# Another order of products in an attention kernel's inner unit, with each key difference placed behind the reader of the one before

## The chip, the core and the metric

The kernel runs on one core of a Trainium2 chip. A core has TensorE (PE: matrix products into PSUM, with its weight loads shown apart as PEld), VectorE (DVE), ScalarE (ACT), GpSimd (POOL) and SyncE (SP, which here issues the DMAs). The engines run their own instruction queues in order and wait for each other at semaphores. The metric is the device time of one execution in microseconds (us), lower is better. A time before is the median of several executions; the profile comes from one more, of which the span from the first to the last instruction is shown.

## What is computed

Four attention layers follow each other on `x` of 2048 tokens by 576 channels, with a layer norm before each and the input added after each. Layers 0 and 2 (kind A) have 32 heads of width 18 with their own keys and values; layers 1 and 3 (kind B) have 32 query heads on one shared key and value.

```python
def _A_ref(x, wqkv, wo):
    qkv = (x @ wqkv).reshape(B, S, 3, H, Dh).transpose(2, 0, 3, 1, 4)
    q, k, v = qkv[0], qkv[1], qkv[2]
    scores = jnp.einsum("bhqd,bhkd->bhqk", q, k) * (Dh ** -0.5)
    p = _softmax(scores, axis=-1)
    o = jnp.einsum("bhqk,bhkd->bhqd", p, v)
    return o.transpose(0, 2, 1, 3).reshape(B, S, D) @ wo
# _B_ref: the same with k = x @ wk and v = x @ wv shared by all heads
x = A_x
x = x + _A_ref(_layernorm(x), A_wqkv, A_wo)
x = x + _B_ref(_layernorm(x), B_wq, B_wk, B_wv, B_wo)
x = x + _A_ref(_layernorm(x), A_wqkv, A_wo)
x = x + _B_ref(_layernorm(x), B_wq, B_wk, B_wv, B_wo)
```

## The kernel before

Each layer projects queries, keys and values, then runs a long attention loop, then the output projection. The attention is done for 16 pairs of heads `p` and 4 blocks `u` of 512 queries, so 64 parts (p, u) per layer and 256 in all. One part needs three kinds of work:

- **Maxima.** 32 products of 128 queries by 512 keys (two heads `a`, four query chunks `qc`, four key blocks `kb`), made by `max_mm` (PE L601). VectorE reads each from PSUM and takes the maximum over the keys (L606). The softmax needs the maximum of each query over all keys; `max_final` (L797) joins them, GpSimd splits the negative in two, and it goes by DMA into two extra rows of the queries.
- **Exponentials.** 32 products of 128 keys by 512 queries, made by `exp_mm` (PE L822), now with the maximum subtracted by the extra rows. ScalarE reads each from PSUM and writes the exponential to a tile `pt` (L826).
- **PV.** Four of these tiles at a time are multiplied with the values into the accumulator `oacc` (PE L864); when all 32 are in, ScalarE copies `oacc` to `oc` (L873).

A **key difference** shares a maximum between two key blocks. For key blocks 0 and 1, max(s0, s1) = s0 + max(s1 - s0, 0). So `max_mm` makes a product with the difference of the two blocks' keys (PE L590), ScalarE takes its relu (L599) and writes it to the one SBUF tile `relu`, and later the product of key block 0 is read by VectorE together with that tile (L604, followed by a short read of its accumulator): sum and maximum in one instruction. This instruction is the **reader** of the difference. It takes one pass off VectorE and gives one to ScalarE, three times per part. There is one `relu` tile, so the next relu may be written only when the reader of the last is done.

The heads of a pair lie in different halves of the array's rows: `q` and `k` are sliced from partition 64 a. Products of different heads that follow each other can run side by side.

**The order** is written out by hand in the table `UNIT`. One pass through its ten rows is a unit, with 32 exponentials and 32 maxima; it runs over and over, across the parts, since the maxima run `LEAD` = 14 steps of four ahead of the exponentials. An item is a letter, a head and a rank: `m` a plain maximum, `r` a key difference, `e` an exponential. The number after a row is how many columns of PV follow the row's products; 512 columns are one step. PV is 928 columns behind (`PV_LAG`).

```python
while m_done[0] < 4 * ns:
    rows, cols = UNIT[phase % len(UNIT)]
    run_todo(LEAD + sum(e_next) / 4)
    for kind, a, rank in rows:
        if kind == "e":
            exp_next(a, rank)
        elif m_done[0] < 4 * ns:
            max_mm(oldest(rank))
    ...
    pv_cols(cols - skip)
```

**Banks.** Beside `oacc` there are seven PSUM banks. `lru` holds them in the order of their last use, and `oldest(rank)` takes the one that was used longest ago (rank 0), or the next (1, 2). A product can start only when the last reader of its bank is done: ScalarE for `e` and `r`, VectorE for `m`. So each item's place and rank also say for which engine, and how far back, PE waits.

**Who reads which difference.** `m_order` fills the 16 maxima of a head in a part: the reader of a difference is the first plain maximum of the same head that stands more than three maxima behind it. Maxima are numbered 0 to 31 in a unit, differences included. Counted so, the table before has differences 13 (row 5, head 1), 18 (row 6, head 0) and 27 (row 9, head 1), with readers 17 (row 6), 22 (row 8) and 31 (row 10).

Other work is issued between the rows by `run_todo`, by how many exponentials have been issued: the transpose of the maxima (L806) and its DMAs, the sums and the division of the output on GpSimd, the loads of the next heads and of weights. `slot` picks a `pt` tile out of a ring of 14; `wrote` and `seen` are its account at build time of which ScalarE writes PE has already waited for, and steer that choice so that an exponential needs few waits.

Of the kernel before, what the change touches and what calls it, by code (L numbers as in the profile page):

```python
# [61 lines left out]

UNIT = [("m10 e00 e00 m10 m01 e10", 448),
# [9 lines left out]
UNIT = [([(o[0], int(o[1]), int(o[2])) for o in rows.split()], cols) for rows, cols in UNIT]  # L75
PV_LAG = 928
UNIT_M = [(kind, a) for rows, _ in UNIT for kind, a, _ in rows if kind != "e"]
assert len(UNIT_M) == 32 and sum(cols for _, cols in UNIT) == 4096


@with_exitstack
def tile_kernel(ctx: ExitStack, tc: tile.TileContext, A_x, A_wqkv, A_wo, B_x, B_wq, B_wk, B_wv, B_wo, out):
# [69 lines left out]
    def bank(i, name):  # L152
        lru.remove(i)
        lru.append(i)
        return psum.tile([P, 512], F32, tag=f"b{i}", bufs=1, name=name)
# [255 lines left out]
    for layer in range(4):  # L411
# [125 lines left out]
        def ops(p):  # L537
            return big[:, q_slot(p)], big[:, k_slot(p)]
# [11 lines left out]
        for a in range(2):  # L550
            n = -4 * LEAD % 32
# [10 lines left out]
        def max_place(a, i):  # L562

            p, u = divmod(i // 16, 4)
            if i < len(m_first):
                return (0, *m_first[i])
            n = i % 16
            return (p, u, *m_order[a][n]) if i >= 32 else (p, u, n // 2 % 4, n // 8 % 2 * 2 + n % 2)
# [5 lines left out]
        def max_mm(bank=mtile):  # L574

            i = m_done[0]
            a = m_heads[i]
            p, u, qc, kb = max_place(a, m_next[a])
            q, k = ops(p)
            if (p, u) not in mxs:  # L580
                mxs[p, u] = pool.tile([P, 32], F32, name="mx") if (p, u) < (0, 2) else mx2[u % 2]
            mx, ps = mxs[p, u], bank("psm")
            by_act = reader[lru[-1]]
            reader[lru[-1]] = False
            b, r = 64 * a, 16 * a + 4 * qc + kb
            c0 = u * 512 + qc * P
            if (p, u) >= (0, 2) and (a, qc, kb) in m_diff:
                assert kd_pair[p % 2 if is_a and p else 2] == (p if is_a else 0)
                k = kd(p)[b:b + 3 * DH]
                nc.tensor.matmul(ps.rearrange("p (h t) -> p h t", h=2) if p == 0 or not is_a else ps,  # L590
                                 q[b:b + 3 * DH, c0:c0 + P], k,
                                 start=True, stop=True)
                t = relus[p, u, a, qc] = relu[:, :512]
                reader[lru[-1]] = True
                if not by_act:
                    seen[0] = max(seen[0], wrote.get("relu", -1))
                wrote["relu"] = ticks[0]
                ticks[0] += 1
                nc.scalar.activation(t, ps, AF.Relu)  # L599
            else:  # L600
                nc.tensor.matmul(ps, q[b:b + KM, c0:c0 + P], k[b:b + KM, kb * 512:(kb + 1) * 512], start=True, stop=True)  # L601
                if kb == 0 and (p, u, a, qc) in relus:
                    t = relus.pop((p, u, a, qc))
                    nc.vector.tensor_tensor_reduce(t, ps, t, 1.0, LOWEST, OP.add, OP.max, mx[:, r:r + 1])  # L604
                else:
                    nc.vector.reduce_max(mx[:, r:r + 1], ps, axis=AX.X)  # L606
            m_next[a] += 1
            m_done[0] += 1
            while m_full and i >= m_full[0][1] + 2:
                max_final(*m_full.pop()[0])  # L610
            m_count[p, u] = m_count.get((p, u), 0) + 1
            if m_count[p, u] == 32:
                assert m_next[0] == m_next[1]
                m_full.append(((p, u), i))

        relus, diffs, kd_pair = {}, {}, {}
        ring, free, wrote, seen, ticks = [], [], {}, [-1], [0]

        def kd(p):
            if p == 0 or not is_a:  # L620
                return big[:, 1::4, 7 * 256:]
            i = p % 2
            return xx_flat[:, 512 * i:512 * i + 512]
# [43 lines left out]
        def max_pairs():  # L667

            if is_a:
                run_todo(m_done[0] // 4)  # L670
            elif m_done[0] == 44:
                max_store(0, 0)
            elif m_done[0] == 48:
                max_rows(0, 0)
            for i in range(4):
                max_mm(etile if i == 3 else mtile)
            while m_full:
                max_final(*m_full.pop()[0])
# [116 lines left out]
        def max_final(p, u):  # L795
            neg = pool.tile([P, 8], F32, name="neg")
            nc.vector.tensor_reduce(neg, mxs.pop((p, u)).rearrange("p (b k) -> p b k", k=4), axis=AX.X, op=OP.max,  # L797
                                    negate=True)
            hl = nms[p, u] = hls[(4 * p + u) % 2]
            copy(nc.gpsimd, hl[:, 0:8], neg)  # L800
            nc.gpsimd.tensor_tensor(hl[:, 8:16], neg, hl.bitcast(F32)[:, 0:8], op=OP.subtract)
# [109 lines left out]


        relu, raw = (pool.tile([P, 640], F32, tag="xh", bufs=2, name=n) for n in ("relu", "raw"))
        todo = {}

        def at(b, f, *args):
# [31 lines left out]
        def run_todo(st):  # L948
            for n in sorted(n for n in todo if n <= st):
                for f, args in todo.pop(n):  # L950
                    f(*args)
# [29 lines left out]
            skip = min(cols, PV_LAG - lagged)  # L981
            lagged += skip
            pv_cols(cols - skip)
            phase += 1
# [47 lines left out]
```

## Time and profile before

| | |
|---|---|
| median of 3 runs | 5727.78 us (5721.95 to 5728.45) |
| the profiled execution | 5725.34 us |
| its span | 5723.6 us |
| granted TensorE clock | 0.999 |
| busy share of the span | PE 98%, DVE 88%, ACT 84%, POOL 32% |
| one unit in layer 1 (2001.47 to 2020.59 us) | 19.12 us, PE 18.76, DVE 18.20, ACT 18.15 busy |

A row of the page's groups names the line, the engine and the operation, output and inputs by their names, the shapes and the count, then the busy time, the mean duration of one in ns, and the idle time before it with what ended it. Instructions of one kind overlap a little, so the busy time is less than count times mean. The view of waits says which engine waited at which line for whom: total, times, longest. The timeline has the start, the length, the engine and the line, with successive instructions of one group merged. A PE instruction's end is modelled.

### The profile page before, as it was taken

Reading aid. Unit: us, or ns where it says so; the run is one execution under the profiler, and the core shown is the slowest. Engines: PE = TensorE matmul, PEld = TensorE weight load, DVE = VectorE, ACT = ScalarE, POOL = GpSimd, SP = SyncE. Lnnn points to the kernel's source line nnn. Section 1 sums busy time; section 2 is a strip of 40 time slices with the busy share of each in tenths; the row PEclk is TensorE's granted clock in tenths of the full one; section 3 lists DMA queues with packets and bytes.
Section 4 is the critical chain, followed back from the end, with each engine's and each line's share of the span. In section 5 each row is a group of like instructions: output and inputs, shape, how many; then the busy total and the mean of one; then the engine's idle time right before and its main releaser. Section 6 shows DMA issues by size and latency. Waiting matters only on the chain.

```text
span 5723.6 us, 143368 instructions
## 1 busy us (share of the span) xinstructions
PE 5606.4 (98%) x55774; PEld 3067.1 (54%) x55774; DVE 5026.7 (88%) x9489; ACT 4831.2 (84%) x9624; POOL 1842.7 (32%) x2396
## 2 busy tenths in 40 slices
PE   9999999999999999999999999999999999999999
PEld 8644444444844444444686444444448444444446
DVE  4799999998699999999737999999977999999995
ACT  2599999999389999999626999999992999999996
POOL 3243333334233333323412433333342332323232
PEclk9999999999999999999999999999999999999999
DMA  6321111111421000000253211111114100000002
GB/s 204 120 59 41 42 46 44 43 44 27 130 62 26 23 24 20 21 23 24 60 172 102 55 46 41 44 44 46 38 38 132 51 24 23 24 24 20 23 15 79
DMA packets 276207, 303.69 MB, mean 53 GB/s; under 512 B 136270, under 2 KB 194214, under 8 KB 266238
## 3 DMA queue, kind: packets, MB, share of 16 engines
q1 hardware_dynamic: 275526, 294.53, 18.0%
q8 instruction: 438, 7.18, 0.5%
q14 instruction: 243, 1.99, 0.1%
HBM read 168.50 MB, written 121.95 MB: 51 GB/s over the span
## 4 chain that ended last, share of the span: by engine, by line
PE 85%; DVE 8%; ACT 3%; issue 2%; POOL 1%; DMA 0%; SPq 0%; ACTq 0%; POOLq 0%; DVEq 0%
PE oacc L864 33%; PE psm L601 21%; PE pse L822 19%; PE psn L259 6%; DVE mx L606 5%; PE psq L433 5%; ACT relu L599 3%; DVE relu L604 3%; PE psm L590 1%; ACT pt L826 0%; POOL ev L445 0%; PE ps L251 0%; DMA big<-qk_d 0%; POOL wsm L205 0%; PE oacc L252 0%
## 5 line engine op out<-in xcount | busy, mean ns | idle before, releaser
L826 ACT ACTIVATE pt<-pse 128x512 f32<-128x512 f32 x8192 | 4233.6, 620 | 104.8 <-PE pse L822 86.0
L606 DVE TENSOR_REDUCE mx<-psm 128x1 f32<-128x512 f32 x6704 | 4183.3, 684 | 81.6 <-PE pse L822 49.0
L601 PE MATMUL psm<-big 62*128 62x512 f32 x7448 | 2461.4, 430 | 91.5 <-ACT relu L599 88.8
L822 PE MATMUL pse<-big 64*128 64x512 f32 x8192 | 2537.5, 442 | 1.7 <-ACT evr L444 1.6
L864 PE MATMUL oacc<-pt,vbuf 128*19 128x416 f32 (+9 forms) x26544 | 1733.0, 368 | 4.6 <-DVE oc L176 4.0
L822 PEld LDWEIGHTS pse<-big 64*128 64x128 f32 x8192 | 1214.0, 184 | 796.8 <-DVE mx L606 370.6
L601 PEld LDWEIGHTS psm<-big 62*128 62x128 f32 x7448 | 1178.7, 185 | 687.2 <-ACT pt L826 251.9
L864 PEld LDWEIGHTS oacc<-pt,vbuf 128*19 128x19 f32 x26544 | 546.4, 97 | 792.4 <-issue 551.9
L176 POOL TENSOR_SCALAR hl<-neg 128x8 fp32r<-128x8 f32 x256 | 50.6, 197 | 2693.1 <-DVE neg L797 2693.1
L604 DVE CUSTOM_DVE_ANT_0 relu<-psm,relu 128x512 f32<-128x512 f32 x744 | 509.4, 685 | 175.7 <-ACT pt L826 173.6
L599 ACT ACTIVATE relu<-psm 128x512 f32<-128x512 f32 x744 | 452.1, 608 | 140.8 <-DVE mx L604 135.2
L864 PE MATMUL oacc<-pt,vy 128*19 128x384 f32 (+3 forms) x8176 | 570.1, 383 | 0.0
L892 POOL TENSOR_TENSOR rl<-lt,mone 128x8 f32<-128x8 f32 x256 | 422.3, 1650 | 297.6 <-DMA lt<-os 291.6
L176 POOL TENSOR_SCALAR os<-oc 32x512 f32<-32x512 f32 x512 | 313.2, 612 | 114.2 <-DVE oc L176 63.6
L441 ACT ACTIVATE ev<-psq 128x512 fp32r<-128x512 f32 (+1 forms) x112 | 66.9, 598 | 326.9 <-PE psq L433 222.8
L883 POOL TENSOR_TENSOR os<-os,oc 96x512 f32<-96x512 f32 x256 | 328.0, 1281 | 21.4
L905 POOL TENSOR_TENSOR os<-os,rb 96x512 f32<-96x512 f32 x256 | 328.7, 1284 | 18.9 <-DMA rb<-r_d 18.9
L259 PE MATMUL psn<-wsm,xx 128*128 128x288 f32 x2240 | 307.9, 296 | 1.3 <-issue 1.3
L259 PEld LDWEIGHTS psn<-wsm,xx 128*128 128x128 f32 x2240 | 298.7, 188 | 14.3 <-issue 12.3
L864 PEld LDWEIGHTS oacc<-pt,vy 128*19 128x19 f32 x8176 | 177.9, 98 | 229.4 <-issue 196.6
L447 DVE TENSOR_TENSOR ev<-psq,ev 128x512 fp32r<-128x512 f32 (+1 forms) x84 | 58.0, 691 | 213.9 <-ACT ev L441 202.6
L433 PE MATMUL psq<-yx,big 128*128 128x512 f32 (+2 forms) x826 | 197.1, 391 | 4.2 <-ACT yx L243 2.2
(93 smaller groups left out, 2391.5 us busy)
## 6 DMA issues: line engine op xcount, KB each, us to landing
big<-qk_d SPq DMA_DIRECT2D x172, 432.0 KB
qk_d<-ev SPq DMA_DIRECT2D x96, 512.0 KB
qk_d<-ev SPq DMA_DIRECT2D x120, 256.0 KB
rb<-r_d SPq DMA_DIRECT2D x512, 36.0 KB
o_d<-os SPq DMA_DIRECT2D x512, 36.0 KB
o<-o_d SPq DMA_DIRECT2D x64, 256.0 KB
xx<-qk_d SPq DMA_DIRECT2D x120, 72.0 KB
big<-m_d SPq DMA_DIRECT2D x512, 4.0 KB
```

The lines of the kernel that those rows point to most:

```text
L176: eng.tensor_scalar(dst, src, 1.0, 0.0, op0=OP.mult, op1=OP.add)
L259: nc.tensor.matmul(ps, lhs[:, xc, :], wsm[:, wc, h * 288:(h + 1) * 288], start=i == 0, stop=i == len(TERMS) - 1)
L433: nc.tensor.matmul(ps[:n].rearrange("p (u t) -> p u t", u=2)[:, us], w[:, wc, :n], xts[T][:, us, xc, :], start=(xc, wc) == TERMS[0], stop= ...
L599: nc.scalar.activation(t, ps, AF.Relu)
L601: nc.tensor.matmul(ps, q[b:b + KM, c0:c0 + P], k[b:b + KM, kb * 512:(kb + 1) * 512], start=True, stop=True)
L604: nc.vector.tensor_tensor_reduce(t, ps, t, 1.0, LOWEST, OP.add, OP.max, mx[:, r:r + 1])
L606: nc.vector.reduce_max(mx[:, r:r + 1], ps, axis=AX.X)
L822: nc.tensor.matmul(e, k[r:r + KE, kc * P:(kc + 1) * P], q[r:r + KE, u * 512:(u + 1) * 512], start=True, stop=True)
L826: nc.scalar.activation(pt, e, AF.Exp, scale=SCALE)
L864: nc.tensor.matmul(oacc[j:j + DH + 1, cs], v_of(kc)[:, 2 * p + a if is_a else 0, :], pts[p, u, i][:, cs], start=kc < 2 and c0 == 0, stop=k ...
L892: nc.gpsimd.tensor_tensor(rl, lts.pop((p, u)), mone, op=OP.pow)
L905: nc.gpsimd.tensor_tensor(t[:96], t[:96], rb[:96], op=OP.mult)
```

## The change

The table `UNIT` is replaced by another of ten rows. Items, ranks and PV columns stand differently; the differences are now 13 (row 5), 20 (row 7) and 28 (row 9), all of head 1. Around it, the one `relu` tile becomes a list of tiles that is taken in turn, with its account kept per tile; the list has one entry. An assertion at build time holds that a tile is not taken again before its reader has been issued.

```diff
@@ -62,16 +62,16 @@
 
 
 
-UNIT = [("m10 e00 e00 m10 m01 e10", 448),
-        ("m00 e11 e00 m10 e10 m01", 480),
-        ("e10 m01 e00 m10 m00 e10", 416),
-        ("e00 m11 m00 m10 e10 e01", 352),
-        ("e00 e10 m00 r12 m10 e01", 384),
-        ("m00 e10 e01 m10 m11 r00", 448),
-        ("e00 m10 e00 m01 e10 m01 e10", 416),
-        ("e10 m00 m10 m10 e00 e10 e00", 416),
-        ("m00 e10 e02 e10 m01 r10 m00", 352),
-        ("m11 e00 e10 m01 m10 e11 e00", 384)]
+UNIT = [("e00 m11 e10 e00 m00 m10", 416),
+        ("e00 e10 m00 m10 m01 e10", 512),
+        ("m10 e00 m01 e10 e10 m01", 384),
+        ("e10 m01 e10 e01 m10 e00", 320),
+        ("m00 e10 m00 r10 m00 e10", 448),
+        ("e00 m10 e00 m00 e10 m01 e10", 416),
+        ("e00 m10 e00 m10 r10 m00 e10", 416),
+        ("e00 m10 e00 m10 m10 e10 e00", 384),
+        ("e10 m00 m00 e00 m11 e00 r10", 416),
+        ("m10 e00 e11 m00 e11 m00", 384)]
 UNIT = [([(o[0], int(o[1]), int(o[2])) for o in rows.split()], cols) for rows, cols in UNIT]
 PV_LAG = 928
 UNIT_M = [(kind, a) for rows, _ in UNIT for kind, a, _ in rows if kind != "e"]
@@ -590,17 +590,20 @@
                 nc.tensor.matmul(ps.rearrange("p (h t) -> p h t", h=2) if p == 0 or not is_a else ps,
                                  q[b:b + 3 * DH, c0:c0 + P], k,
                                  start=True, stop=True)
-                t = relus[p, u, a, qc] = relu[:, :512]
+                j = turn_r[0] = (turn_r[0] + 1) % len(relu)
+                assert all(n != j for n, _ in relus.values())
+                t = relu[j][:, :512]
+                relus[p, u, a, qc] = j, t
                 reader[lru[-1]] = True
                 if not by_act:
-                    seen[0] = max(seen[0], wrote.get("relu", -1))
-                wrote["relu"] = ticks[0]
+                    seen[0] = max(seen[0], wrote.get(-1 - j, -1))
+                wrote[-1 - j] = ticks[0]
                 ticks[0] += 1
                 nc.scalar.activation(t, ps, AF.Relu)
             else:
                 nc.tensor.matmul(ps, q[b:b + KM, c0:c0 + P], k[b:b + KM, kb * 512:(kb + 1) * 512], start=True, stop=True)
                 if kb == 0 and (p, u, a, qc) in relus:
-                    t = relus.pop((p, u, a, qc))
+                    _, t = relus.pop((p, u, a, qc))
                     nc.vector.tensor_tensor_reduce(t, ps, t, 1.0, LOWEST, OP.add, OP.max, mx[:, r:r + 1])
                 else:
                     nc.vector.reduce_max(mx[:, r:r + 1], ps, axis=AX.X)
@@ -613,7 +616,7 @@
                 assert m_next[0] == m_next[1]
                 m_full.append(((p, u), i))
 
-        relus, diffs, kd_pair = {}, {}, {}
+        relus, diffs, kd_pair, turn_r = {}, {}, {}, [0]
         ring, free, wrote, seen, ticks = [], [], {}, [-1], [0]
 
         def kd(p):
@@ -911,6 +914,7 @@
 
 
         relu, raw = (pool.tile([P, 640], F32, tag="xh", bufs=2, name=n) for n in ("relu", "raw"))
+        relu = [relu]
         todo = {}
 
         def at(b, f, *args):
```

## Prediction

> **What bounds it.** The page comes first. No engine is free, and the chain that ended last runs through TensorE with a share on the other two.
>
> ```profile
> span 5723.6 us, 143368 instructions
> PE 5606.4 (98%) x55774; PEld 3067.1 (54%) x55774; DVE 5026.7 (88%) x9489; ACT 4831.2 (84%) x9624; POOL 1842.7 (32%) x2396
> PE oacc L864 33%; PE psm L601 21%; PE pse L822 19%; PE psn L259 6%; DVE mx L606 5%; PE psq L433 5%; ACT relu L599 3%; DVE relu L604 3%; PE psm L590 1%; ACT pt L826 0%; POOL ev L445 0%; PE ps L251 0%; DMA big<-qk_d 0%; POOL wsm L205 0%; PE oacc L252 0%
> L873 ACT ACTIVATE oc<-oacc 128x512 f32<-128x512 f32 x248 | 149.9, 605 | 0.7 <-issue 0.7
> ```
>
> ScalarE's copy `oc` comes once a unit: 248 units. The table by stretches, cut at five periods of the timeline, gives one: 19.12 us, of which PE 18.76, DVE 18.19 and ACT 18.16 are busy. That is 248 x 19.12 = 4742 us, four fifths of the span; only it changes.
>
> ```profile
> 2001.47:2020.59 19.12, 18.76 (x204) 9.24 (x201) 18.20 (x35) 18.15 (x38) 5.79 (x7) 1.00 0.05 11
> sum 95.60, PE 93.82 PEld 46.53 DVE 90.93 ACT 90.80 POOL 28.95; mean PE 18.76 PEld 9.31 DVE 18.19 ACT 18.16 POOL 5.79
> ```
>
> The view of waits says what the period contains beside work (us in total, times, longest):
>
> ```profile
> ACT relu L599 <- DVE mx L604: 135.2, 241, 0.6
> PE psm L601 <- ACT relu L599: 88.8, 244, 0.7
> DVE relu L604 <- ACT pt L826: 173.6, 246, 0.7
> ```
>
> All three fall about once a unit, so they are one event: ScalarE's relu waits 0.56 us for a VectorE reader, PE 0.36 us for that relu's bank, and VectorE then 0.71 us for PE. The timeline of one unit shows it:
>
> ```profile
> 2001.47 0.50 PE L601 MATMUL psm<-big 62*128 62x512 f32 x1
> 2002.01 1.29 DVE L606 TENSOR_REDUCE mx<-psm 128x1 f32<-128x512 f32 x2
> 2002.05 0.46 PE L590 MATMUL psm<-big 54*128 54x512 f32 x1
> 2003.22 0.68 DVE L604 CUSTOM_DVE_ANT_0 relu<-psm,relu 128x512 f32<-128x512 f32 x1
> 2003.33 0.50 PE L822 MATMUL pse<-big 64*128 64x512 f32 x1
> 2004.00 0.60 ACT L599 ACTIVATE relu<-psm 128x512 f32<-128x512 f32 x1 [0.56 <-DVE mx L604]
> 2004.65 0.50 PE L601 MATMUL psm<-big 62*128 62x512 f32 x1 [0.36 <-ACT relu L599]
> 2005.91 0.18 PEld L822 LDWEIGHTS pse<-big 64*128 64x128 f32 x1 [0.69 <-ACT pt L826]
> 2007.87 0.50 PE L601 MATMUL psm<-big 62*128 62x512 f32 x1
> 2009.73 0.50 PE L601 MATMUL psm<-big 62*128 62x512 f32 x1
> 2011.82 0.50 PE L601 MATMUL psm<-big 62*128 62x512 f32 x1
> 2011.82 0.50 PE L822 MATMUL pse<-big 64*128 64x512 f32 x1
> 2013.60 0.50 PE L601 MATMUL psm<-big 62*128 62x512 f32 x1
> 2015.44 0.49 PE L822 MATMUL pse<-big 64*128 64x512 f32 x1
> 2017.16 0.50 PE L822 MATMUL pse<-big 64*128 64x512 f32 x1
> 2018.91 0.50 PE L822 MATMUL pse<-big 64*128 64x512 f32 x2
> 2020.59 0.50 PE L601 MATMUL psm<-big 62*128 62x512 f32 x1
> ```
>
> The PE lines at 2001.47, 2003.33, 2005.91, 2007.87 and so on are the first products of the table's rows 6, 7, 8, 9, 10, 1, 2, 3, 4, 5 and again 6. Row 5's key difference (index 13) is read by index 17, the last maximum before row 6's key difference (18, at 2002.05). With one relu buffer, relu 18 must wait for reader 17, which has two maxima ahead of it on VectorE; row 7's index 21 (2004.65) takes relu 18's bank.
>
> **What a row costs PE without waits.** The two lines at 2011.82 show two products of different heads side by side; I count such a pair as one slot. Rows of 3 slots last 1.78 (row 1, 448 columns), 1.84 (row 2, 480) and 1.72 (row 3, 416); rows of 4 last 1.96 (row 8, 416) and 1.86 (row 9, 352). So 64 columns cost 0.10 to 0.12, a slot about 0.23. Rows 4 and 10 by the same steps are 1.61 and 1.91, row 5 is 1.68 as measured, row 6 equals row 1, row 7 equals row 8: together 18.10. The period's other 1.02 is waiting: row 7 lasts 2.58 (0.62 over), row 10 2.09 (0.18), row 4 1.75 (0.14), row 6 1.86 (0.08). Row 10's is the relu again, as ScalarE runs without a pause from 2004.00 until then. PE's idle 0.36 is therefore a poor measure of the loss; the rows give 0.62 to 0.80.
>
> **The change, part by part.** The Python edits around `relu` give a list of length one: same buffer, no new instruction, 0. The new table has the same ten rows, 32 exponentials, 26 plain maxima, 3 relus, 3 readers and 4096 columns, and counted by heads again 34 slots (six rows of 3, four of 4). So PE's floor stays 18.10, and so do the loads of DVE and ACT. All that changes is who waits for whom.
>
> Removed: the close reader. New key differences are 13, 20 and 28, all of head 1; by the order rule their readers are 18, 24 and, in the next unit, 0. The reader stands two products ahead of the next difference (18 before 20), then four (24 before 28), then thirteen; before it was one. Between row 6's start and relu 20, ScalarE has six exponentials; reader 18 has a transpose and three maxima ahead of it.
>
> Added: other bank waits. Four kinds of step decide them:
>
> ```profile
> 2004.49 5.58 ACT L826 ACTIVATE pt<-pse 128x512 f32<-128x512 f32 x11
> 2012.36 6.13 DVE L606 TENSOR_REDUCE mx<-psm 128x1 f32<-128x512 f32 x10 [0.19 <-PE pse L822]
> 2019.51 1.08 ACT L826 ACTIVATE pt<-pse 128x512 f32<-128x512 f32 x2 [0.24 <-PE pse L822]
> 2001.79 0.20 DVE L806 STREAM_TRANSPOSE tr<-hl 128x32 f32<-128x32 f32 x1
> 2018.40 0.17 DVE L797 TENSOR_REDUCE neg<-mx 128x8 f32<-128x32 f32 x1
> 2018.50 2.48 DVE L606 TENSOR_REDUCE mx<-psm 128x1 f32<-128x512 f32 x4
> ```
>
> ScalarE starts one item each (5.58 - 0.61)/10 = 0.497, call it 0.495 with relus; VectorE one maximum each (6.13 - 0.68)/9 = 0.606, a reader takes 0.68, the transpose 0.22 (2001.79 to 2002.01), `neg` 0.10 (2018.40 to 2018.50). A first product reaches ScalarE 0.59 after the row's start (2018.91 to 2019.51) and VectorE 0.54 after (2011.82 to 2012.36), later slots 0.23 each. A bank is free 0.05 after its reader ends (2004.60 to 2004.65). After a held last product the next row starts 1.26 later with 416 columns (2004.65 to 2005.91), so 0.57 plus the columns' 0.69.
>
> **The loop that is late next.** Set 0 where row 1's last product `m10` starts. Row 2 starts at 1.26, its first maximum at 1.26 + 0.54 + 0.23 = 2.03. From there VectorE has seven maxima and `neg` before row 4's `m10`, which starts at 2.03 + 7 x 0.606 + 0.10 = 6.37 and frees its bank at 7.10. Row 5's last product `e10` takes that bank. Row 4's last, `e00`, waits for row 3's last exponential too, behind the `oc` copy, so PE comes to row 5 at about 6.6 and would start `e10` at about 7.05. Row 6 starts at 7.10 + 0.57 + 0.75 (448 columns) = 8.42, and its first exponential at 9.01. Rows 6 to 10 give ScalarE 4, 4, 4, 4 and 3 items; the last starts at 9.01 + 18 x 0.495 = 17.92, ends 0.61 later, and its bank is free at 18.58. Row 1's `m10` takes it. So the unit can't be shorter than 18.58. Inside this loop row 9's `r10` waits for row 8's last exponential: by the same steps it holds PE by up to 0.13, and ScalarE's row 10 begins 0.04 to 0.10 later. I take **18.65**.
>
> The walk puts relu 20 at 11.93 + 0.05 and its reader's release at 11.77 + 0.05: a margin of 0.15, no wait. Relus 28 and 13 have over 1 us. PV of row 6 needs row 6's second exponential in its last 32 columns: 0.2 of margin. Table-driven DMA starts move by one row at most, and `neg` and the transpose stay in their rows; POOL, busy 5.79 of 19.12, covers this. If that cover went, one row's delay of an issue still lies under the 14 steps of lead. Waits that need a second semaphore cost an instruction on their own; their number in the new order is not known:
>
> ```profile
> L599 ACTq EVENT_SEMAPHORE  x492: 17/17/17, 228.4 to 5618.7; - x164
> L822 PEldq EVENT_SEMAPHORE  x506: 51/51/573, 214.3 to 5640.5; - x169
> ```
>
> One PE one more or less per unit is 0.05, both ends +-13 us; I take 0, and the range holds it.
>
> **Sum.** 19.12 - 18.65 = 0.47 per unit, times 248 = 117 us. The profiled execution took 5725.3 us (span 5723.6), between the runs of 5721.95 and 5728.45, 2.4 under the median. 5725.3 - 117 = 5609. A tenth of a us per unit is 25 us.
>
> **Rivals.**
> *Larger holds.* The same seven banks serve a tighter schedule, and 0.55 of holds may be 0.8 to 0.95 when several in a unit add (rows 4, 5, 7, 9 and 1 each show up to 0.2 in the walk). Period 18.9 to 19.05: 5671 to 5708. For it: the old table lost 0.22 in rows 4 and 6, away from the relu. Against: those holds lie on one loop and don't all add.
> *Nothing gained.* The wait is only handed to another reader of the same banks: 19.12, 5725. The Trainium skill, in "Perfetto Trace Analysis", section "Optimization Strategy", says that a gap which repeats on the engine that should be saturated can mean too few buffers. By that rule a new order with the same buffers would leave the 0.36. Against it stands the row at 2004.00, where a reader's place in the queue ends the wait, not a missing bank.
> *More.* All holds vanish and the busiest engine's 18.19 (DVE) to 18.4 decides: 19.12 - 18.3 = 0.82, 5522, or 5495 to 5547. Against: the 18.58 loop.
> *Slower.* Reader 18 comes late on VectorE. The margin is 0.15; ScalarE's next items feed row 8's last slot and row 9 without slack, so beyond the margin the period grows one for one, and passes 19.12 when the reader is 0.15 + 0.47 = 0.62 late, which is one maximum (0.606) more ahead of it. With relu 20 waiting the old 0.56 the unit takes 19.21: 5748. For it: VectorE is the fullest beside PE. Against: the order counted in the code.
>
> **Chances.** Forecast (18.45 to 18.85) 0.66; larger holds 0.12; nothing gained 0.06; more 0.08; slower 0.08. That is faster 0.86, same 0.06, slower 0.08, where 0.2% (11 us) is about what a measurement of this kernel tells from no change. The range, 5560 to 5685, runs from a period of 18.45 to 18.96: it takes in the semaphore instructions and half of the larger holds.
>
> **What would show it.** Right: relu's wait for DVE under 30 us in total (135.2 before), PE's for relu gone, a period near 18.65 in the table by stretches, DVE and ACT busy still 18.2, and PE or ACT waits left at rows 1, 4, 5 and 9. Wrong: a relu wait of about 0.5 per unit at row 7, or busy sums per unit that changed.

## The result, and the profile after

The changed kernel takes 5563.37 us (median of 4 runs, 5561.36 to 5564.3) against 5725.64 for the kernel before, measured with it: a ratio of 0.9716, 95% interval 0.97 to 0.9733. It is 162 us faster. The forecast was 5609, a gain of 117, with a range from 5560 to 5685.

From the page of the kernel before: the chain that ended last by engine, and the groups of the readers and of the relus.

```profile
PE 85%; DVE 8%; ACT 3%; issue 2%; POOL 1%; DMA 0%; SPq 0%; ACTq 0%; POOLq 0%; DVEq 0%
L604 DVE CUSTOM_DVE_ANT_0 relu<-psm,relu 128x512 f32<-128x512 f32 x744 | 509.4, 685 | 175.7 <-ACT pt L826 173.6
L599 ACT ACTIVATE relu<-psm 128x512 f32<-128x512 f32 x744 | 452.1, 608 | 140.8 <-DVE mx L604 135.2
```

From the page of the changed kernel: the span, the busy times, the same chain, and the same two groups (now L607 and L602).

```profile
span 5561.7 us, 139390 instructions
PE 5531.2 (99%) x53790; PEld 3103.8 (56%) x53790; DVE 5008.5 (90%) x9489; ACT 4808.8 (86%) x9624; POOL 1843.3 (33%) x2396
PE 95%; issue 1%; POOL 1%; DMA 1%; DVE 1%; SPq 0%; ACT 0%; POOLq 0%; ACTq 0%; DVEq 0%
L607 DVE CUSTOM_DVE_ANT_0 relu<-psm,relu 128x512 f32<-128x512 f32 x744 | 509.5, 685 | 38.0 <-PE psm L604 6.9
L602 ACT ACTIVATE relu<-psm 128x512 f32<-128x512 f32 x744 | 480.1, 645 | 1.4 <-DVE mx L607 0.7
```

The work of DVE and ACT is what it was (same counts, busy within 0.5%). Their shares of the chain fall from 8% and 3% to 1% and 0%; PE has 95% instead of 85%. The relus' idle time before them fell from 140.8 us to 1.4, the readers' from 175.7 to 38.0.

One thing did change in the work, which the prediction had put at nothing: PE runs 53790 matmuls instead of 55774, eight fewer a unit, since by the new columns fewer row ends cut a step of PV in two (16 pieces a unit instead of 17). A run below that has the old table's 55774 (two relu tiles) is as fast, so the gain doesn't come from that.

In the view of waits (total, times, longest) one relu waits for a reader instead of 241, and PE's wait for a relu is no longer there:

```profile
ACT relu L602 <- DVE mx L607: 0.7, 1, 0.7
```

The table by stretches gives two units of the changed kernel. One takes 18.45 us instead of 19.12, with DVE and ACT busy for 18.09 and 18.06:

```profile
2111.30:2129.75 18.45, 18.45 (x196) 9.43 (x192) 18.09 (x35) 18.06 (x37) 5.79 (x8) 1.00 0.05 11
2129.75:2148.20 18.45, 18.45 (x196) 9.42 (x192) 18.09 (x35) 18.06 (x37) 5.79 (x8) 1.00 0.15 36
```

19.12 - 18.45 is 0.67, and 248 units of it are 166 us; the profiled executions differ by 5725.34 - 5563.46 = 162. The missing 4 us were not followed up.

The timeline of the first of the two (start, length, engine and line) has the rows' first products and the few instructions that the text comes back to: reader 18 and relu 20 in row 7, the last exponentials of rows 10 and 3, row 1's `m10`, row 4's last exponential product, VectorE's first maximum of row 2 and its `m10` of row 4, and row 5's `e10` at 2130.33:

```profile
2111.30 0.50 PE L604 MATMUL psm<-big 62*128 62x512 f32 x1
2113.10 0.50 PE L825 MATMUL pse<-big 64*128 64x512 f32 x1
2115.07 0.50 PE L825 MATMUL pse<-big 64*128 64x512 f32 x1
2115.74 0.69 DVE L607 CUSTOM_DVE_ANT_0 relu<-psm,relu 128x512 f32<-128x512 f32 x1
2116.63 0.60 ACT L602 ACTIVATE relu<-psm 128x512 f32<-128x512 f32 x1
2117.06 0.49 PE L825 MATMUL pse<-big 64*128 64x512 f32 x1
2118.98 0.49 PE L825 MATMUL pse<-big 64*128 64x512 f32 x1
2121.00 0.50 PE L604 MATMUL psm<-big 62*128 62x512 f32 x1
2122.53 0.61 ACT L829 ACTIVATE pt<-pse 128x512 f32<-128x512 f32 x1
2122.69 0.49 PE L825 MATMUL pse<-big 64*128 64x512 f32 x1
2123.26 0.43 PE L604 MATMUL psm<-big 62*128 62x512 f32 x2
2124.45 0.50 PE L825 MATMUL pse<-big 64*128 64x512 f32 x2
2125.22 0.69 DVE L609 TENSOR_REDUCE mx<-psm 128x1 f32<-128x512 f32 x1
2126.34 0.50 PE L604 MATMUL psm<-big 62*128 62x512 f32 x1
2127.98 0.62 ACT L829 ACTIVATE pt<-pse 128x512 f32<-128x512 f32 x1
2128.01 0.50 PE L825 MATMUL pse<-big 64*128 64x512 f32 x1
2128.65 0.50 PE L825 MATMUL pse<-big 64*128 64x512 f32 x1
2129.51 0.68 DVE L609 TENSOR_REDUCE mx<-psm 128x1 f32<-128x512 f32 x1
2129.75 0.50 PE L604 MATMUL psm<-big 62*128 62x512 f32 x1
2130.33 0.41 PE L825 MATMUL pse<-big 64*128 64x512 f32 x1
```

The row starts at 2111.30, 2113.10, 2115.07, 2117.06, 2118.98, 2121.00, 2122.69, 2124.45, 2126.34, 2128.01 and 2129.75 are rows 5 to 10, 1 to 4 and again 5. They last 1.80, 1.97, 1.99, 1.92, 2.02, 1.69, 1.76, 1.89, 1.67 and 1.74. By the steps of the prediction these rows without waits would last 1.78, 1.96, 1.96, 1.91, 1.96, 1.67, 1.72, 1.89, 1.67 and 1.56, together 18.08. So 0.18 of hold is left in row 4, 0.06 in row 9 and no more than 0.04 elsewhere. Relu 20 starts 0.20 after its reader is done (2115.74 + 0.69 = 2116.43).

### The profile page after: what moved, and what is told of

It is laid out like the page before. It is cut to its first block, busy times and chain, and to the rows that moved or that the text cites. A ratio compares the mean times of both kernels' runs of the same rounds, so it can differ in the third digit from the quotient of the medians.

```text
span 5561.7 us, 139390 instructions
## 1 busy us (share of the span) xinstructions
PE 5531.2 (99%) x53790; PEld 3103.8 (56%) x53790; DVE 5008.5 (90%) x9489; ACT 4808.8 (86%) x9624; POOL 1843.3 (33%) x2396
## 3 DMA queue, kind: packets, MB, share of 16 engines
q14 instruction: 243, 1.99, 0.1%
## 4 chain that ended last, share of the span: by engine, by line
PE 95%; issue 1%; POOL 1%; DMA 1%; DVE 1%; SPq 0%; ACT 0%; POOLq 0%; ACTq 0%; DVEq 0%
PE oacc L867 37%; PE pse L825 28%; PE psm L604 16%; PE psn L259 6%; PE psq L433 5%; PE psm L590 2%; DVE mx L609 0%; POOL ev L445 0%; PE ps L251 0%; POOL wsm L205 0%; DMA raw<-in_A_wo_dram 0%; ACT pt L829 0%; DMA qk_d<-ev 0%; POOL big L205 0%; DMA big<-m_d 0%
## 5 line engine op out<-in xcount | busy, mean ns | idle before, releaser
L825 PE MATMUL pse<-big 64*128 64x512 f32 x8192 | 2605.8, 441 | 4.2 <-DMA big<-m_d 3.4
L604 PE MATMUL psm<-big 62*128 62x512 f32 x7448 | 2366.7, 432 | 4.1 <-ACT evr L444 1.6
L867 PE MATMUL oacc<-pt,vbuf 128*19 128x384 f32 (+10 forms) x25552 | 1733.9, 376 | 3.7 <-DVE oc L176 3.7
L825 PEld LDWEIGHTS pse<-big 64*128 64x128 f32 x8192 | 1162.0, 184 | 872.9 <-ACT pt L829 345.4
L867 PE MATMUL oacc<-pt,vy 128*19 128x288 f32 (+8 forms) x7184 | 569.0, 413 | 0.0
L607 DVE CUSTOM_DVE_ANT_0 relu<-psm,relu 128x512 f32<-128x512 f32 x744 | 509.5, 685 | 38.0 <-PE psm L604 6.9
L602 ACT ACTIVATE relu<-psm 128x512 f32<-128x512 f32 x744 | 480.1, 645 | 1.4 <-DVE mx L607 0.7
L867 PEld LDWEIGHTS oacc<-pt,vy 128*19 128x19 f32 x7184 | 154.5, 98 | 176.5 <-issue 132.8
```

Of the source, the lines that this page charges most:

```text
L825: nc.tensor.matmul(e, k[r:r + KE, kc * P:(kc + 1) * P], q[r:r + KE, u * 512:(u + 1) * 512], start=True, stop=True)
L867: nc.tensor.matmul(oacc[j:j + DH + 1, cs], v_of(kc)[:, 2 * p + a if is_a else 0, :], pts[p, u, i][:, cs], start=kc < 2 and c0 == 0, stop=k ...
```

## The experiments

The theory: the old table lost its time because one relu waited for the reader of the last, by the time at which VectorE's queue reached it. The rivals: the gain comes from the new order of banks, heads and columns; or what counts is how many products lie between reader and difference. Each ratio is to the kernel before, measured beside the run; its medians there lie between 5723.00 and 5727.19 us, so times of different runs compare to about 4 us.

**The old table, reader one maximum earlier.** Only the rule that picks readers is changed, in the kernel before.

```diff
-                order[min(j for j, (at_, x) in enumerate(own) if at_ > own[i][0] + 3 and not x and not order[j])] = qc, 0
+                order[min(j for j, (at_, x) in enumerate(own) if at_ > own[i][0] + 2 and not x and not order[j])] = qc, 0
```

> The kernel before with its old table; only the rule that picks readers is changed from more than three maxima behind to more than two. Reader 17 of difference 13 becomes 16, one maximum (0.61 us) earlier on VectorE; readers 21 and 31 as good as before. Table, banks, heads and PV columns are the old ones. Theory (the gain comes from the relu's wait for its reader): the wait of 0.56 per unit goes, with row 7's 0.62 and most of row 10's 0.18; unit 18.3 to 18.5 us, time 5530 to 5580, relu's wait for VectorE under 10 us. Rival (the gain comes from the new order of banks and heads, the wait is only handed on): unit above 18.9, time 5670 to 5725.

Measured: 5589.26 us (5587.66 to 5590.08), ratio 0.9761 (0.9746 to 0.9775). That is 135 of the 162 us, without the new table. It is 9 us above the expected range. In its timeline, the first line is the reader, the second ScalarE's item before the relu, the third the relu that had waited:

```profile
2125.32 0.68 DVE L604 CUSTOM_DVE_ANT_0 relu<-psm,relu 128x512 f32<-128x512 f32 x1
2125.51 0.64 ACT L826 ACTIVATE pt<-pse 128x512 f32<-128x512 f32 x1
2126.11 0.60 ACT L599 ACTIVATE relu<-psm 128x512 f32<-128x512 f32 x1
```

The relu starts 0.11 after its reader's end (2126.00), about the 0.10 of the old wait (2003.90 to 2004.00): it still starts as soon as its reader lets it. No idle time is listed, since it starts before the item ahead of it ends (2126.15). But it starts 0.60 after that item's start, where relu 20 of the changed kernel does so 0.48 after (2116.15 to 2116.63). That is some 0.12 lost in each unit, by estimate 30 us if all of it shows (248 x 0.12); the next run, without this wait, is 30.5 us faster.

**The old table with two relu tiles.** The code of the changed kernel, the old table, and a second tile.

```diff
-        relu = [relu]
+        relu = [relu, xx_flat[:, 4096:4608]]
```

> The old table with the old readers, and a second relu tile taken in turn (512 columns of a buffer that is idle in the attention loop; relus written there are rounded to its type, which changes the maximum that is subtracted in its last bits). Reader 17 stays directly ahead of difference 18, but relu 18 goes to the other tile. Theory (the wait is for the one tile's reader): the wait goes, unit 18.50 to 18.56 as with the reader one maximum earlier, time 5580 to 5600. Rival (the reader matters in another way than by the tile, for instance by the banks it holds): unit above 18.9, time over 5670.

Measured: 5558.74 us (5556.43 to 5562.13), ratio 0.9708 (0.9691 to 0.9724): as fast as the changed kernel, and 21 us under the lower expected end. The view of ScalarE's waits has no relu any more. The table by stretches shows the unit:

```profile
2106.01:2124.43 18.42, 18.42 (x210) 9.51 (x200) 18.09 (x36) 18.08 (x37) 5.80 (x7) 1.00 0.05 11
```

With the old order of items, banks and columns (and the old count of 55774 matmuls), this run has the whole gain. The new table is therefore not needed for it: it is one way to a relu that doesn't wait.

**The new table, all readers later.** The reverse of the first run, in the changed kernel.

```diff
-                order[min(j for j, (at_, x) in enumerate(own) if at_ > own[i][0] + 3 and not x and not order[j])] = qc, 0
+                order[min(j for j, (at_, x) in enumerate(own) if at_ > own[i][0] + 5 and not x and not order[j])] = qc, 0
```

> The changed kernel with its new table; only the rule is changed from more than three maxima behind to more than five. Reader 18 of difference 13 becomes 19, one maximum later on VectorE; the readers of 20 and 28 become 27 and 34 (2 in the next unit), both still ahead of the next difference. In the trace relu 20 starts 0.20 after its reader 18 is done. Theory: relu 20 now waits 0.61 - 0.20 = 0.4 per unit, and as ScalarE's next items feed rows 8 and 9 without slack, nearly all of it shows: unit 18.75 to 18.85, time 5640 to 5665. Rival (slack around it absorbs the wait, the order of banks is what counts): 5563 to 5580.

Measured: 5767.71 us (5766.3 to 5769.2), ratio 1.0072 (1.0055 to 1.0088): slower than the kernel before, 204 us over the changed one, twice what was expected. The waits show two relu waits per unit, not one:

```profile
ACT relu L602 <- PE pse L825: 84.1, 218, 0.7
ACT relu L602 <- DVE mx L607: 66.4, 243, 0.4
```

The second line is relu 20, which waits for reader 19. The first is relu 28: its reader had become 27, the maximum just ahead of it in the same row, and in the timeline it starts 0.10 after that reader's end. The view gives it to PE, whose product came in that time too. The expectation had overlooked this neighbour.

**Only the first reader later.** This run separates the two.

```diff
-... if at_ > own[i][0] + 3 and ...
+... if at_ > own[i][0] + (3 if qc else 5) and ...
```

> The changed kernel; only the first difference's reader moves, from 18 to 19 (one maximum, 0.61 us, later on VectorE); 20 and 28 keep readers 24 and 32. In the run with all readers later there were two waits in a unit, at relu 20 (0.28) and at relu 28, whose reader had become 27 directly ahead of it, and the unit was 0.85 longer (19.29 against 18.44). Theory: one wait of 0.3 to 0.4 is left, at relu 20, and row 8 is held by about as much: unit 18.75 to 18.90, time 5640 to 5680. Rival (the two waits were one chain, or the wait at relu 20 alone is absorbed): unit up to 18.55, time under 5595.

Measured: 5652.66 us (5650.99 to 5656.59), ratio 0.9873 (0.986 to 0.9887), 89 us over the changed kernel, as expected. Its waits, and row 7 and the start of row 8 in its timeline:

```profile
ACT relu L602 <- DVE mx L607: 67.3, 243, 0.4
```

```profile
2112.69 0.49 PE L825 MATMUL pse<-big 64*128 64x512 f32 x1
2113.77 0.61 ACT L829 ACTIVATE pt<-pse 128x512 f32<-128x512 f32 x1
2113.86 0.68 DVE L607 CUSTOM_DVE_ANT_0 relu<-psm,relu 128x512 f32<-128x512 f32 x1
2114.64 0.60 ACT L602 ACTIVATE relu<-psm 128x512 f32<-128x512 f32 x1 [0.27 <-DVE mx L607]
2115.29 0.18 PEld L604 LDWEIGHTS psm<-big 62*128 62x128 f32 x1 [0.30 <-ACT relu L602]
```

The relu starts 1.95 after row 7 (2112.69 to 2114.64); in the changed kernel it was 1.56 (2115.07 to 2116.63). It is 0.39 later, and 89 us by 248 units are 0.36: nearly one for one. The wait that the view shows (0.27) is less than the delay. ScalarE itself is not late, its item before the relu starts 1.08 after row 7 in both kernels (2113.77 here, 2116.15 there); but the view counts only from that item's end (2114.38), and an undisturbed relu starts 0.11 before it (2116.63 against 2116.74). The last line is row 8's bank, which waits for that relu.

**The difference right behind its reader.** In the new table's row 7, difference 20 and the maximum ahead of it change places.

```diff
-        ("e00 m10 e00 m10 r10 m00 e10", 416),
+        ("e00 m10 e00 r10 m10 m00 e10", 416),
```

> The changed kernel with the new table; row 7's difference changes places with the plain maximum in front of it (20 becomes 19), so that its product comes right behind reader 18 in PE's order, as close as in the old table. Its place among ScalarE's items, and the reader's place among VectorE's, stay. Theory (what counts is the time at which each queue gets there, not how many products lie between): relu's wait stays under 10 us in total, time 5563 within 15 us. Rival (the distance in products counts): the wait of about 0.5 per unit comes back, 5660 to 5690.

Measured: 5577.45 us (5576.19 to 5578.95), ratio 0.974 (0.9726 to 0.9755): 14 us over the changed kernel. ScalarE's relus wait 0.3 us in total. So the number of products between is not what counts; both queues' times are. The 14 us are at the edge of what was allowed. Their place is row 1: in a regular unit (18.50 instead of 18.45) it lasts 1.80 instead of 1.75. The lines are row 10's last exponential and row 1's last two products:

```profile
2036.40 0.60 ACT L829 ACTIVATE pt<-pse 128x512 f32<-128x512 f32 x1
2037.07 0.48 PE L604 MATMUL psm<-big 62*128 62x512 f32 x2
```

One of the two, `m10`, takes the bank of that exponential, which is free at 2036.40 + 0.60 + 0.05 = 2037.05, just as the product comes. In the changed kernel the same bank is free 0.07 earlier than needed.

**What holds the unit at 18.45.** Four runs took up the rest. The first leaves out the accumulator's copy, the second moves `neg` (the short VectorE reduction that joins a part's maxima) one maximum later, the third does both, the fourth keeps all work, moves `neg` and shifts columns.

```diff
-                if m_done[0] < 4 * ns:
+                if (p, u) == (0, 0):
                     nc.scalar.activation(oc, oacc, AF.Copy)
+                elif m_done[0] < 4 * ns:
+                    pass
```

> The changed kernel without ScalarE's copy of the finished accumulator, except for the first part of each layer; the sums and the output then work on old data, in the same instructions. It leaves out 0.5 us of ScalarE per unit and the wait of row 3's PV for it. Theory (row 4's hold of 0.18 comes from the copy that stands ahead of row 3's exponentials on ScalarE): row 4 lasts 1.56 to 1.60 instead of 1.74, the unit 18.15 to 18.27, time 5490 to 5520. Rival (the hold comes from VectorE or from PE itself): 5555 to 5563.

Measured: 5563.19 us (5559.76 to 5565.12), no change. Row 4 did lose its hold, but the time came back in row 5:

```profile
2128.55 0.50 PE L825 MATMUL pse<-big 64*128 64x512 f32 x1
2130.05 2.54 DVE L609 TENSOR_REDUCE mx<-psm 128x1 f32<-128x512 f32 x4
2130.16 0.50 PE L604 MATMUL psm<-big 62*128 62x512 f32 x1
2130.78 0.49 PE L825 MATMUL pse<-big 64*128 64x512 f32 x1
2132.09 0.50 PE L825 MATMUL pse<-big 64*128 64x512 f32 x1
```

Row 4 lasts 1.61 (2128.55 to 2130.16) instead of 1.74, row 5 1.93 instead of 1.80. Row 5's last product starts at 2130.78. Its bank belongs to row 4's last maximum, the first of the four that VectorE starts at 2130.05: 2130.05 + 0.68 + 0.05 = 2130.78. In the changed kernel the same bank is free at 2129.51 + 0.73 = 2130.24, 0.09 before `e10` starts (2130.33). So a second limit stood just behind the first, and taking the first away left the second.

```diff
-            while m_full and i >= m_full[0][1] + 2:
+            while m_full and i >= m_full[0][1] + 3:
```

> The changed kernel; the joining of a part's maxima (the short reduction neg, 0.10 us of VectorE) is issued one maximum later, behind row 4's last maximum instead of ahead of it, so it leaves the stretch of VectorE that row 5's last product waits for. Theory (two holds of about the same size reach row 5: VectorE's stretch, and ScalarE's copy of the accumulator by row 4's last product): alone it is worth 0.00 to 0.05 per unit, since row 4's hold of 0.18 stays: time 5551 to 5563. Rival (VectorE's stretch alone sets the unit): 0.10 per unit, 5536 to 5542.

Measured: 5561.12 us (5557.87 to 5562.3), ratio 0.9711 (0.9698 to 0.9725): 2 us less than the changed kernel, which the intervals don't tell apart. As the theory said, it is not worth 0.10 by itself.

> The kernel without ScalarE's copy of the accumulator (but for the first part of each layer; the output then works on old data) and with neg one maximum later. Without the copy alone row 4 lost its hold (1.74 to 1.61) and row 5 got one (1.81 to 1.93), and the time stayed. Theory (VectorE's stretch from row 2 to row 4's last maximum takes over, and goes on by way of row 6 and ScalarE to row 1): with both gone the unit is 18.32 to 18.36, time 5530 to 5545. Rival (row 5's hold is something else, or another loop of the same length stands behind): 5555 to 5563.

Its edit is the two above together. Measured: 5546.83 us (5545.16 to 5549.23), ratio 0.9688 (0.9675 to 0.9701). That is 14 to 16 us less than either alone: the two do stand side by side. It is 2 us above the expected range; row 5 lasts 1.85, where 1.78 would be without waits, so a part of its hold stays.

```diff
-        ("m10 e00 m01 e10 e10 m01", 384),
-        ("e10 m01 e10 e01 m10 e00", 320),
+        ("m10 e00 m01 e10 e10 m01", 448),
+        ("e10 m01 e10 e01 m10 e00", 256),
...
-            while m_full and i >= m_full[0][1] + 2:
+            while m_full and i >= m_full[0][1] + 3:
```

> The changed kernel, all work kept: neg one maximum later, and 64 columns of PV moved from row 4 (320 to 256) to row 3 (384 to 448), so that row 4 starts 0.11 later against row 3's exponentials and its last product meets less of a hold. Theory: row 4's hold shrinks from 0.18 to about 0.07 and row 5's stays away: unit 18.34 to 18.38, time 5535 to 5550. Rival (as in the run before): 5555 to 5566.

Measured: 5575.0 us (5570.2 to 5578.82), ratio 0.9736 (0.9723 to 0.9749): the theory failed, it is 12 us slower. Row 4 lasts 1.52, and would last 1.46 without waits, so its hold did shrink. But row 5 lasts 1.95 instead of 1.80, since its last `m00` now waits (last line). The first lines are row 4's first product and row 4's first and third exponential on ScalarE:

```profile
2113.81 0.50 PE L825 MATMUL pse<-big 64*128 64x512 f32 x1
2114.34 0.60 ACT L829 ACTIVATE pt<-pse 128x512 f32<-128x512 f32 x1
2115.32 0.61 ACT L829 ACTIVATE pt<-pse 128x512 f32<-128x512 f32 x1
2115.97 0.18 PEld L604 LDWEIGHTS psm<-big 62*128 62x128 f32 x1 [0.31 <-ACT pt L829]
```

`m00` takes the bank of the third exponential, which is free 2.17 after row 4 began (2115.32 + 0.61 + 0.05 - 2113.81). With row 4 at 1.52 and 0.57 to a row's third pair of products, PE would be there after 2.09. The copy has no part in it, since ScalarE was done with row 3 at 2114.30 (2113.68 + 0.62), before row 4's first exponential: row 4 with fewer columns is too short for its own exponentials.

**Other tables.** Three more tables were worked out with these sizes, to bring the holds down with all work kept. Each has `neg` one maximum later. The first two differ in every row; the third keeps the first two rows' columns.

```diff
+UNIT = [("e10 m00 e00 m10 m01 e10", 368),
+        ("e11 m01 e00 m10 e00 m11", 352),
+        ("e10 m01 e10 e00 m11 m00", 480),
+        ("m01 e10 m11 e00 e00 e10", 448),
...
```

> All work kept; neg one maximum later and another table, in which the differences (14th, 20th and 28th or so of the unit's maxima) keep their readers early on VectorE, and after the accumulator's copy ScalarE has fewer items that a row's last product waits for. Theory (holds of rows 1, 4, 5, 7 and 9 are bank waits, of the sizes measured so far): unit 18.30 to 18.36 against 18.44, time 5530 to 5548. Rival (a new order brings other holds of the same size): 5555 to 5575.

> As the run before, with a table that shares no row with it. Theory: the same unit, 18.30 to 18.36, time 5530 to 5548. Rival: 5555 to 5575.

Measured: 5911.63 us (5910.7 to 5914.57), ratio 1.0323 (1.0308 to 1.0339), and 5907.59 (5905.59 to 5909.16), ratio 1.0315 (1.03 to 1.0331): some 360 us over the expected range. The waits and the timeline of the first show a wait that was not in the reckoning:

```profile
PE oacc L867 <- ACT oc L876: 299.5, 244, 1.3
```

```profile
2116.87 0.55 PE L867 MATMUL oacc<-pt,vbuf 128*19 128x208 f32 x8
2117.99 0.62 ACT L876 ACTIVATE oc<-oacc 128x512 f32<-128x512 f32 x1
2118.65 0.65 PE L867 MATMUL oacc<-pt,vbuf 128*19 128x272 f32 x8 [1.23 <-ACT oc L876]
```

PV starts 928 columns late. Where the first rows' columns add up to 928, as 448 + 480 and 416 + 512 do, a part's accumulator ends with a row's end, and its copy runs beside the next row's products. Here it ends 208 columns into row 3, and the other 272 stand behind ScalarE's queue until the copy is done; ScalarE and VectorE then idle 1.21 and 1.08 us until the next row's products come. In the second table the wait is 300.0 us, 244 times.

```diff
+UNIT = [("m12 e02 m11 e00 e11 m00", 416),
+        ("m02 e10 m10 e00 e11 m00", 512),
+        ("e10 m00 e01 m11 e10 m00", 368),
+        ("e00 m12 e00 m10 e01 e10", 288),
+        ("m01 e12 m01 r10 e10 m00", 432),
+        ("e11 m00 e10 e10 m00 e01 m10", 432),
+        ("e01 m11 r12 e01 e00 m11 m00", 416),
+        ("e11 m00 m10 e02 e10 r10 m00", 416),
+        ("e00 m11 m00 m10 e00 e00 e10", 416),
+        ("e10 m01 e00 e12 m11 m00", 400)]
```

> All work kept; neg one maximum later and a third other table, in which the first two rows again have 416 and 512 columns, so that the end of a part's accumulator falls on the end of row 2 as in the tables before and after. In the two runs with other tables it fell inside a row, and the rest of that row's PV stood 1.2 us behind ScalarE's copy of the accumulator. Theory (those tables were slow by that alone, and the bank waits are as worked out): unit 18.28 to 18.36, time 5525 to 5548, PE's wait for the copy gone. Rival (their bank waits were worked out wrongly): 5580 or more.

Measured: 5564.71 us (5560.42 to 5566.57), ratio 0.9719 (0.9706 to 0.9732). PE's wait for the copy is gone. The items differ too, so this is not a test of the boundary alone; but that wait is 300 of the 344 to 348 us that the two slow tables have over the changed kernel. The hoped-for 18.3 did not come (18.43): it is as fast as the changed kernel. No run with all work kept is clearly below it: the lowest is the old table with two tiles, 5558.74.

## Why the prediction was right, and where it was off

The gain was 162 us where 117 were forecast. The time is only 3 us inside the lower end of the range, and the unit of 18.45 is the lowest that the forecast took in.

**The event.** Right. The three waits of 0.56, 0.36 and 0.71 us were one event, its cause was the place of reader 17 on VectorE, and it is what the change removed: one maximum earlier for that reader brings 135 us, a second tile all of it.

**The loss read from the rows, not from PE's idle time.** Right. PE's idle 0.36 would have given 89 us. The rows gave 0.62 to 0.80, the unit lost 0.67. But row 10's 0.18 was put down to the relu too, and most of it wrongly: with the reader moved, row 10 of the old table still lasts 2.08 to 2.11, and with two tiles 2.03 or 2.04, against 2.09.

**The unchanged loads.** Right for DVE and ACT, which are busy for 18.09 and 18.06 per unit, 0.1 under the old 18.19 and 18.16. PE has eight matmuls fewer a unit, which the prediction didn't count and which no run shows to be worth anything.

**The margin at relu 20.** Right in that there is no wait, but smaller than the forecast 0.15: the relu starts 0.20 after its reader's end, and a relu that has waited starts 0.10 after it, so 0.10 is left to spare. The run with only the first reader later agrees: its reader ends 1.85 after row 7's start instead of 1.36, which is 0.49 later, and the relu is 0.39 later. The price past the margin, one for one, was right (0.39 of delay, 0.36 of unit). The rival "slower" is real, as the run with all readers later shows (1.0072), but from a base of 18.45 it took two such waits and not one.

**The loop that is late next.** This is the step that was mis-sized, and the claim made of it fails: "the unit can't be shorter than 18.58", against 18.45. Its links by the timeline above:

- from row 1's `m10` (2123.26) to row 2 (2124.45) 1.19, forecast 1.26;
- to VectorE's first maximum of row 2 (2125.22) 0.77, as forecast;
- from there until the bank of row 4's `m10` is free (2129.51 + 0.73) 5.02, forecast 5.07;
- from row 5's `e10` (2130.33) to row 6 (2113.10, so 2131.55 a unit later) 1.22, forecast 1.32;
- from row 6 to ScalarE's last item of row 10 (2122.53) 9.43, forecast 9.50;
- from there until its bank is free (2123.19) 0.66, as forecast.

Together they are 18.29 where 18.58 was forecast. The rest of the 18.45 is slack: `e10` starts 0.09 after its bank is free, and `m10` 0.07 after. So in the changed kernel this loop holds nothing. The walk took both products for held ones and charged PE's later restart (1.26 to the next row instead of 1.19, 1.32 instead of 1.22), which did not come, and it took the steps of VectorE and ScalarE 0.05 and 0.07 too long. Row 9's hold, for which 0.07 was given on top, is 0.06.

What the traces show in its place is the other hold that the walk named: row 4's last product, behind the accumulator's copy. Row 3's last exponential ends at 2127.98 + 0.62 = 2128.60, the product that takes its bank starts 0.05 later (2128.65), and row 4 lasts 0.18 longer than it would without waits. The unit is the 18.08 of the rows, this 0.18, row 9's 0.06 and 0.13 in pieces of at most 0.04. The forecast loop stands close behind: without the copy row 5's `e10` does wait for its bank, and with the difference moved in row 7 row 1's `m10` comes just as its bank is freed.

**The rule on buffers.** The prediction weighed the sentence of the Trainium skill in "Perfetto Trace Analysis", section "Optimization Strategy", that a repeating gap can mean too few buffers, as a reason for no gain. The runs show both sides: the gap did come from a single buffer, the relu tile (5558.74 with two), and an order that keeps the same buffers closed it too (5563.37).

**Open.** Why orders as different as the changed table, the third other table and the old one with two tiles all end at 18.42 to 18.45 is not settled. Without the copy and with `neg` later the unit falls by 0.07 (18.38), so the holds in rows 4 and 5 are a part of it; the small holds in rows 7, 9 and 10 were not tried.

## What to carry to other kernels

Where an engine must wait until another has read a shared tile, count what stands ahead of both in their own queues; the number of instructions between them in the program says little, and one place in the slower queue (0.61 us here) can decide 100 us. When three engines are each 95% busy, read the loss from the lengths of comparable rows and not from the bottleneck's idle time, and expect that a removed hold can be met by the next one, as here. In an order written by hand, look for what the old one keeps silently, such as an accumulator that ends where a row ends, before changing it.

## What was not expected of the hardware

A relu whose product has long been ready still starts about 0.10 us after the reader it depends on (2003.90 to 2004.00 before, 2126.00 to 2126.11 in the first run). Where ScalarE runs without a pause, an item starts about 0.11 before the one ahead of it ends (2116.63 against 2116.74 in the changed kernel), so a delay of up to that size costs time without being listed as a wait.
